# Fourier stage over all 576 tokens at once: no reversed copies through DRAM, one load of each image's rows

## The chip, the cores and the metric

One core of a Trainium2 chip runs the whole program: attention, then a Fourier layer with an MLP, then a gated MLP. The number that counts is the device time of one execution in microseconds (us); three runs of the kernel before took 1231.2, 1236.0 and 1241.24, median 1236.0. Engines are called by the profile's names: PE (TensorE matmul), DVE (VectorE), ACT (ScalarE), POOL (GpSimd) and SP, whose queue issues most DMAs.

## What is computed

The part that the change touches is the mixing at the head of the second layer. `x` is the attention's output, 4 images of 576 tokens by 512 features:

```
X = np.fft.fft(x, axis=1)
X = np.fft.fft(X, axis=2)
u = x + np.real(X).astype(np.float32)
mu, var = mean and variance of u over the features
un = (u - mu) / np.sqrt(var + 1e-06)
x2 = u + np.maximum(un @ w_ch1, 0.0) @ w_ch2
```

The attention before it (4 images, 8 heads, 576 tokens, head size 64, a bias from a small network on the distances) and the gated MLP behind it keep their code.

## The kernel before

**Attention.** `attention_phase` walks 16 head pairs (4 of each image) of 9 units each; a step `d` handles two units. The steps are written as a software pipeline: scores and their maximum at `d`, exponentials one step later, then a split of the probabilities into two fp16 halves (`high` on ACT, `low` on POOL, line 473), a DMA transpose (`turn`, line 485, on SP's queue) three steps later, and the product with v (`back`, line 527) six steps later. In every third step, and in the last three, PE does the transpose instead (`flip`, with a leftover subtraction `flip_low` on DVE). When a pair is done, `store` writes 128 of the 512 features of one image to a DRAM buffer `xd[b]` (lines 572 and 573).

**The Fourier stage's input.** Before the cosine and sine sums over the tokens are taken, token s is added to and subtracted from token 576 - s, so that 289 rows are contracted. [...] Image 2 goes to a tile of its own (`fx`), image 3 reuses image 0's.

**Folds.** `Folds.prep` is the elementwise work of one image, ten steps: sum and difference of the two row sets (lines 781 and 782, POOL and DVE), the same over the features (787), then four groups of 128 columns, each rounded to the matmul's format by ACT (812), with the remainder taken by POOL (813) and DVE (793). `first_folds` starts it while the attention drains, `fft_phase` calls one step of it at a time between matmuls.

**The two contractions.** `stage1` makes one column group of one image with 7 matmuls of 290 columns against the table `tt` (line 887); an image has five groups: `p1` (one column), `pe`, `po`, `me`, `mo`. `second` contracts the features in 12 or 8 matmuls (line 920), `residual` transposes x itself (lines 906 and 908), and two DVE additions write the result into `ut` (lines 924 and 931). `residual` has two PSUM buffers, and each is freed by one of these additions. Both phases stand under `manual_schedule`; the order on each engine is settled when the program is built. Weight blocks of the MLP (`w<-in_w_ch`) are converted in between by `Weights.step`, 8 short DVE instructions for each.

Of the kernel before, what the change touches and what calls it, by code (L numbers as in the profile page):

```python
# [20 lines left out]
DM = 512  # L21
# [32 lines left out]
REV = 14  # L54
# [296 lines left out]
def attention_phase(tc, nc, io, vs, bias, biasl, raw, xd, ident, after, es, right):  # L351
# [4 lines left out]
    vp = right.enter_context(pool(tc, name="vp", bufs=1, side="right"))  # L356
# [69 lines left out]
    def total(u):  # L426
        n, t, h = units[u]
        sc = live.pop(u)
        bv = bias[t // 2][:, t % 2, 2 * pairs[n][1] + h] if t < 4 else biasl[:, pairs[n][1]]
        s = wp.tile([128, S], F32, tag="s", name="s", bufs=SB)  # L430
# [13 lines left out]
        live[u] = s  # L444
# [87 lines left out]
    def finish(u):  # L532
# [3 lines left out]
        if n not in xs:  # L536
            xs[n] = xp.tile([128, 5, 128], F32, tag="x", name="x")
# [26 lines left out]
    def store(u):  # L564
        n, t, h = units[u]
        if t < 4:
            return
# [10 lines left out]
    wp = es.enter_context(pool(tc, name="att", bufs=3))  # L578
    xp = es.enter_context(pool(tc, name="xs", bufs=2))
# [65 lines left out]
def phases(tc, nc, io, vs, low, raw, xd, ident, tables, after, right):  # L645
# [4 lines left out]
    with ExitStack() as es:  # L650
        att = attention_phase(tc, nc, io, vs, bias, biasl, raw, xd, ident, after, es, right)
# [25 lines left out]
LEAD = 2  # L677
F_LOAD = -3
F_WAIT = 2
F_PREP = 1  # L680
F_STEPS = 2
F_MAX = 7
YB = 3
XPLAN = {10: 1, 14: 1, 30: 1, 31: 1, 32: 1}
AFTER = (0,)


def clear(eng, x):

    eng.memset(x[96:128, :, 2], 0.0)  # L690
    eng.memset(x[0:1, 1, 0], 0.0)


def fetch(eng, x, d):


    f = slice(1, DM + 1)
    eng.dma_start(out=x[:, 0, 0:2, f], in_=d[0:256].rearrange("(k p) d -> p k d", p=128))
    yield
    eng.dma_start(out=x[1:128, 1, 0, f], in_=d[577:704])  # L700
    eng.dma_start(out=x[:, 1, 1, f], in_=d[704:832])
    yield
    for y, s in enumerate((256, 832)):
        r = d[s : s + 32].rearrange("(a s) d -> a s d", a=1)
        eng.dma_start(out=x[0:96, y, 2, f], in_=r.to_broadcast([3, 32, DM]))
    eng.dma_start(out=x[96:98, 0, 2, f], in_=d[288:289].to_broadcast([2, DM]))
    yield


def tables(tc, nc, io, es):  # L710

    cp = es.enter_context(pool(tc, name="dft", bufs=1, side="right"))

# [5 lines left out]
    def load():  # L719
        nc.gpsimd.dma_start(out=tt, in_=io["c_t"])  # L720
# [10 lines left out]
class Folds:  # L731
# [5 lines left out]
    SIZE = 2 * 3 * (DM + 2)  # L737
    WORK = 6144

    def __init__(self, tc, nc, xd, xs, work, es):  # L740
        self.tc, self.nc, self.xd, self.es = tc, nc, xd, es
        self.xs = [self.view(x) for x in xs]
        n = 0

        def room(y, f):
            nonlocal n
            n += y * f
            return work[:, n - y * f : n].rearrange("p (y f) -> p y f", y=y)

        self.eo = [room(3, DM) for _ in range(2)]  # L750
        self.pm = room(12, 256).rearrange("p (y z t) f -> p y z t f", y=2, z=2)
# [3 lines left out]
        self.loads = {}  # L755

    def view(self, x):
        return x.rearrange("p (y t f) -> p y t f", y=2, t=3)

    def open(self):  # L760

        p = self.es.enter_context(pool(self.tc, name="ff", bufs=1, side="right"))
        for x in range(2):
            self.hi.append(p.tile([128, 3, DM], F32R, name=f"fhi{x}"))
            self.lo.append(p.tile([128, 2, DM], F32R, name=f"flo{x}"))
        self.xs.append(self.view(p.tile([128, self.SIZE], F32, name="fx2")))

    def load(self, b, eng=None):

        nc, x = self.nc, self.xs[b % 3]  # L770
        if b < 3:
            clear(nc.gpsimd, x)
        if b == B - 1:
            reverse(nc, self.xd, b)
            yield
        yield from fetch(eng or nc.sync, x, self.xd[b])

    def prep(self, b):
        nc, x, f = self.nc, self.xs[b % 3], slice(1, DM + 1)
        eo, pm, hi, lo = self.eo, self.pm, self.hi[b % 2], self.lo[b % 2]  # L780
        nc.gpsimd.tensor_tensor(out=eo[0], in0=x[:, 0, :, f], in1=x[:, 1, :, f], op=ALU.add)
        nc.vector.tensor_tensor(out=eo[1], in0=x[:, 0, :, f], in1=x[:, 1, :, f], op=ALU.subtract)
        yield

        def half(y, z):
            eng = nc.gpsimd if (y, z) == (1, 1) else nc.vector
            eng.tensor_tensor(
                out=pm[:, y, z], in0=eo[y][:, :, 255::-1], in1=eo[y][:, :, 256:512], op=ALU.subtract if z else ALU.add
            )

        def low(g):
            q, r = slice(128 * g, 128 * g + 128), slice(64, 97)
            nc.vector.tensor_tensor(out=hi[r, 2, q], in0=F[r, 2, q], in1=hi[r, 2, q].bitcast(F32), op=ALU.subtract)

        half(1, 0)
        half(1, 1)
        yield
        half(0, 0)
        yield
        half(0, 1)  # L800
        yield
        F = eo[0]
# [3 lines left out]
        for g, (y, z, op, c) in enumerate(((0, 0, ALU.add, 0), (1, 0, ALU.subtract, 128), (0, 1, ALU.subtract, 0), (1, 1, ALU.add, 128))):  # L806
            q = slice(128 * g, 128 * g + 128)
            o = F[:, :, q]
            s = pm[:, y, z]
            nc.vector.tensor_tensor(out=o[:, :, 1:128], in0=s[:, :, up], in1=s[:, :, dn], op=op)  # L810
            nc.vector.tensor_copy(out=o[:, :, 0:1], in_=pm[:, g // 3, z, :, c : c + 1])
            nc.scalar.activation(out=hi[:, :, q], in_=o, func=AF.Copy)
            nc.gpsimd.tensor_tensor(out=lo[:, :, q], in0=o[:, 0:2], in1=hi[:, 0:2, q].bitcast(F32), op=ALU.subtract)
            if g:
                low(g - 1)
            yield
        low(3)
        yield

    def steps(self):  # L820
        for b in range(B):
            for n, _ in enumerate(self.prep(b)):
                self.done = 10 * b + n
# [5 lines left out]


def first_folds(folds):

    def flow():
        yield from folds.load(0)
        for _ in range(F_WAIT):
            yield
        yield from folds.load(1)

    steps = flow()

    def after(n):
        if n == 0:
            folds.open()
        if n >= F_LOAD:
            next(steps, None)
        for _ in range(F_STEPS):
            if n >= F_PREP and folds.done < F_MAX:
                next(folds.flow)
        if n == LAGS[-1] + 1:
            for _ in steps:  # L850
                pass
# [4 lines left out]
def fft_phase(tc, nc, folds, tabs, ut, bank, extra, es):  # L856
# [9 lines left out]
    COS, SIN = (0, 2, 8), (4, 6, 9)  # L866
# [3 lines left out]
    def load(b):  # L870
        for _ in folds.load(b):
            pass

    need(2)
    need(8)
    load(2)
    need(9 + LEAD)

    def stage1(b, nm, col, ncol, t):
# [3 lines left out]
        seq = [(hi[0:98, 2, c], tt[0:98, t[2]])]  # L883
        for k in range(2):
            seq += [(hi[:, k, c], tt[:, t[0] + k]), (hi[:, k, c], tt[:, t[1] + k]), (lo[:, k, c], tt[:, t[0] + k])]
        for n, (st, mv) in enumerate(seq):
            nc.tensor.matmul(out=y[0:ncol, 0:TP], lhsT=st, rhs=mv, start=(n == 0), stop=(n == 6))
# [4 lines left out]
    def first(b, nm):  # L892
        if nm == "p1":
            x = xs[b % 3]
            nc.scalar.activation(out=x[:, :, :, 0:1], in_=x[:, :, :, 256:257], func=AF.Copy)
        need(10 * b + dict(p1=6, pe=6, po=6, me=7, mo=8)[nm])
        stage1(b, nm, *dict(p1=(128, 1, COS), pe=(0, 128, COS), po=(128, 128, SIN), me=(256, 128, COS), mo=(384, 128, SIN))[nm])

    def residual(b, e, y):
        x = xs[b % 3]  # L900
        t = ps_x.tile([128, 2, 512], F32, tag="xs", name="xs")
        for s in range(2):
            col = 257 + e if s else e
            c = slice(col, col + 255, 2)
            for k in range(2):
                nc.tensor.transpose(t[:, s, 128 * k : 128 * k + 128], x[:, y, k, c], ident)
            r = slice(64, 97)
            nc.tensor.transpose(t[:, s, 256:289], x[r, y, 2, c], ident[r, r])
# [20 lines left out]
    def mirror(b, e):  # L929
        o = ut[:, 2 * e : 2 * e + 2, S * b : S * b + S]  # L930
        ends[0] = nc.vector.tensor_tensor(
            out=o[:, :, T2:S], in0=Ds["xr"][:, :, 287:0:-1], in1=Ds["d"][:, ::-1, 287:0:-1], op=ALU.add
# [3 lines left out]

    def step():
        nonlocal count
        count += 1
        next(folds.flow, None)  # L940
# [6 lines left out]
    for b in range(B):  # L947
        for e in range(2):
# [4 lines left out]
            for n, nm in enumerate(group):  # L953
# [12 lines left out]
        if b + 3 < B:  # L966
            load(b + 3)
# [617 lines left out]
def build(tc, io, out):  # L1585
    nc = tc.nc
    with ExitStack() as ctx:
# [9 lines left out]
        xd = [dp.tile([S + S // 2, DM], F32, name=f"xd{b}") for b in range(B)]  # L1597
        n, m = Folds.SIZE, Folds.WORK
# [150 lines left out]
```

## Time and profile before

| | |
|---|---|
| median of 3 runs | 1236.0 us (1231.2 to 1241.24) |
| profiled execution | 1236.24 us, span 1234.4 us |
| bias tables | 0 to about 125 us |
| attention, up to the last scores | about 125 to 423 us |
| drain of the attention and image 0 of the Fourier stage | 423 to 500 us |
| the rest of the Fourier stage | 500 to 568 us |
| MLP | 568 to 1016 us |
| gated MLP | 1016 to 1234 us |
| busy share of the span | PE 87%, DVE 61%, ACT 46%, POOL 35% |

The profile is of one execution, and 1.8 us lie outside its span. Busy shares are averages over stages with different limits: PE is busy for 331 of 336 us in the middle of the MLP, and for 12 of 30 us between 470 and 500. A stage is therefore read from its own stretch.

### The profile page before, as it was taken

Reading aid. Unit: us, or ns where it says so; the run is one execution under the profiler, and the core shown is the slowest. Engines: PE = TensorE matmul, PEld = TensorE weight load, DVE = VectorE, ACT = ScalarE, POOL = GpSimd, SP = SyncE. Lnnn points to the kernel's source line nnn. Section 1 sums busy time; section 2 is a strip of 40 time slices with the busy share of each in tenths; the row PEclk is TensorE's granted clock in tenths of the full one; section 3 lists DMA queues with packets and bytes.
Section 4 is the critical chain, followed back from the end, with each engine's and each line's share of the span. In section 5 each row is a group of like instructions: output and inputs, shape, how many; then the busy total and the mean of one; then the engine's idle time right before and its main releaser. Section 6 shows DMA issues by size and latency. Waiting matters only on the chain.

```text
span 1234.4 us, 25635 instructions
## 1 busy us (share of the span) xinstructions
PE 1069.7 (87%) x10379; PEld 980.0 (79%) x10379; DVE 749.8 (61%) x2099; ACT 565.2 (46%) x1056; POOL 434.8 (35%) x345
## 2 busy tenths in 40 slices
PE   4989898959868625788788999999999999999998
PEld 2778787858857613567787999999999998898997
DVE  5898877748747535867999723423448427534422
ACT  2788888859857501325444312212224324334332
POOL 2667677757756423431555000000005311101010
PEclk7899999989979868778999999999999999999999
DMA  6442198878878762201543000000013200001001
GB/s 146 155 130 87 32 176 173 170 147 166 177 139 171 128 102 82 96 22 52 158 151 119 1 2 1 1 1 1 35 36 127 59 1 1 18 18 43 1 35 43
DMA packets 145642, 98.86 MB, mean 80 GB/s; under 512 B 111476, under 2 KB 125168, under 8 KB 145396
## 3 DMA queue, kind: packets, MB, share of 16 engines
q1 hardware_dynamic: 142656, 89.84, 31.5%
q10 hardware_dynamic: 2724, 5.90, 1.6%
q8 instruction: 81, 1.33, 0.5%
q0 software_dynamic: 144, 1.48, 0.3%
q14 instruction: 37, 0.30, 0.1%
HBM read 60.64 MB, written 11.79 MB: 59 GB/s over the span
## 4 chain that ended last, share of the span: by engine, by line
PE 50%; DVE 20%; DMA 11%; POOL 7%; SPq 4%; ACT 4%; issue 4%; ACTq 0%; POOLq 0%; DVEq 0%
PE h L1297 12%; PE acc L1333 12%; PE psp L1468 5%; DMA pt<-hl 4%; PE pu L1443 4%; PE po L1490 3%; POOL hl L473 3%; PE pv L1391 3%; PE sc L421 3%; DVE wsq L1033 2%; DVE wsq L1038 2%; SPq L485 2%; DVE wsq L1026 2%; PE bps L265 2%; DMA raw<-in_k 2%
## 5 line engine op out<-in xcount | busy, mean ns | idle before, releaser
L1045 POOL TENSOR_TENSOR wl<-wsq,wh 128x512 fp32r<-128x512 f32 x44 | 80.8, 1848 | 342.4 <-DVE w L1219 249.9
L1297 PE MATMUL h<-uh,wl 128*128 128x256 f32 x576 | 164.1, 286 | 11.2 <-POOL wl L1045 11.2
L1333 PE MATMUL acc<-gh,wh 128*128 128x256 f32 x576 | 164.5, 286 | 3.5 <-ACT gh L1301 3.4
L1297 PE MATMUL h<-uh,wh 128*128 128x256 f32 x576 | 163.1, 285 | 4.4 <-ACT uh L1207 3.2
L1333 PE MATMUL acc<-gl,wh 128*128 128x256 f32 x576 | 162.4, 282 | 5.1 <-DVE gl L1302 4.8
L1297 PE MATMUL h<-ul,wh 128*128 128x256 f32 x576 | 163.2, 284 | 0.0
L1333 PE MATMUL acc<-gh,wl 128*128 128x256 f32 x576 | 161.5, 281 | 0.0
L1302 DVE SCALAR_TENSOR_TENSOR gl<-h,gh 128x256 fp32r<-128x256 f32 x144 | 60.4, 421 | 160.4 <-ACT gh L1301 160.2
L527 PE MATMUL po<-vp,pt 128*128 128x65 f16 (+1 forms) x2240 | 96.3, 198 | 63.9 <-DMA pt<-hl 57.4
L1301 ACT ACTIVATE gh<-h 128x256 fp32r<-128x256 f32 x144 | 54.5, 379 | 210.3 <-PE h L1297 210.1
L527 PEld LDWEIGHTS <-pt 128*128 128x128 f16 (+1 forms) x2240 | 82.5, 103 | 79.0 <-DMA pt<-hl 65.3
L1297 PEld LDWEIGHTS h<-uh,wl 128*128 128x128 f32 x576 | 111.3, 193 | 12.7 <-POOL wl L1045 12.6
L473 POOL TENSOR_TENSOR hl<-P,hl 128x1024 f16<-128x1024 f32 x92 | 116.2, 1287 | 8.3 <-issue 5.7
L1297 PEld LDWEIGHTS h<-uh,wh 128*128 128x128 f32 x576 | 111.1, 194 | 5.4 <-ACT uh L1207 3.7
L1333 PEld LDWEIGHTS acc<-gl,wh 128*128 128x128 f32 x576 | 109.8, 191 | 6.8 <-DVE gl L1302 6.5
L1333 PEld LDWEIGHTS acc<-gh,wh 128*128 128x128 f32 x576 | 109.9, 191 | 5.0 <-ACT gh L1301 4.6
L1297 PEld LDWEIGHTS h<-ul,wh 128*128 128x128 f32 x576 | 111.3, 194 | 0.2 <-DVE ul L1208 0.2
L1333 PEld LDWEIGHTS acc<-gh,wl 128*128 128x128 f32 x576 | 109.7, 190 | 0.0
L456 ACT ACTIVATE P<-s,mm 128x576 f32<-128x576 f32 x144 | 103.3, 765 | 8.7 <-DVE mm L449 8.3
L434 DVE CUSTOM_DVE_ANT_0 s<-sc,lowa 128x576 f32<-128x576 f32 x64 | 48.4, 757 | 49.9 <-PE sc L421 48.3
L265 PE MATMUL bps<-g,mask 128*128 128x64 f16 x1152 | 63.6, 199 | 17.3 <-DVE mask L320 11.1
L248 ACT ACTIVATE mask<-pre 128x576 f16<-128x576 f32 x96 | 60.9, 651 | 35.2 <-PE pre L245 34.1
(257 smaller groups left out, 2837.9 us busy)
## 6 DMA issues: line engine op xcount, KB each, us to landing
w<-in_w_ch SPq DMA_DIRECT2D x32, 512.0 KB
vld<-in_v ACTq DMA_DIRECT2D x16, 320.0 KB
raw<-in_v SPq DMA_DIRECT2D x16, 320.0 KB
raw<-in_q SPq DMA_DIRECT2D x16, 288.0 KB
raw<-in_k SPq DMA_DIRECT2D x16, 288.0 KB
xd<-x SPq DMA_DIRECT2D x16, 256.0 KB
w<-in_w_in SPq DMA_DIRECT2D x8, 512.0 KB
out<-o SPq DMA_DIRECT2D x16, 256.0 KB
```

The lines of the kernel that those rows point to most:

```text
L248: nc.scalar.activation(out=m.rearrange("p (x e) -> p x e", x=2), in_=p[:, :, 0:288], func=AF.Sigmoid, scale=1e30)
L265: nc.tensor.matmul(out=full(ps, it // 2)[:, it % 2, :, gi], lhsT=ms[gi][:, 128 * it : 128 * it + 128], rhs=g[:, k], start=(k == 0), stop=( ...
L456: nc.scalar.activation(out=P[:, x], in_=s, func=AF.Exp, bias=mm[:, 1, x : x + 1], scale=1.0)
L473: nc.gpsimd.tensor_tensor(out=hl[:, :, o : o + c], in0=P[:, :, j : j + c], in1=hl[:, :, j : j + c], op=ALU.subtract)
L527: nc.tensor.matmul(out=po[c, t % 4, 0:w], lhsT=pt[:, x, c], rhs=vp[:, j, hh, f : f + w], start=(i == 0), stop=(i == len(seq) - 1),)
L1045: nc.gpsimd.tensor_tensor(out=lo, in0=w[4], in1=hi.bitcast(F32), op=ALU.subtract)
L1297: nc.tensor.matmul(out=h[:, 0:MC], lhsT=st[:, q], rhs=mv[:, k], start=(n == 0), stop=(n == 11))
L1301: nc.scalar.activation(out=gh, in_=h[:, 0:MC], func=AF.Relu)
L1302: nc.vector.scalar_tensor_tensor(out=gl, in0=h[:, 0:MC], scalar=0.0, in1=gh.bitcast(F32), op0=ALU.max, op1=ALU.subtract)
L1333: nc.tensor.matmul(out=acc[d][:, x], lhsT=st[:, q], rhs=mv, start=(i == LAGF and n == 0), stop=(i == len(items) + LAGF - 1 and n == 2),)
L1443: nc.tensor.matmul(out=p[:, 0:CH], lhsT=st[:, q], rhs=mv[:, kk, e], start=(n == 0), stop=(n == 11))
L1468: nc.tensor.matmul(out=p[:, 0:CH], lhsT=st, rhs=mv, start=(n == 0), stop=(n == len(seq) - 1))
```

## The change

`stage1` contracts all 576 tokens in natural order: 4 blocks of 128 rows and one of 64, with 14 matmuls of 290 columns for each column group instead of 7. The fold over tokens, the reversed copies and the loads of reversed rows go. One image is loaded by two DMAs, `[128, 4 x 512]` and `[64, 512]`; image 0 three steps ahead of the attention's end, images 1 and 2 right behind its last step, each into a tile of its own, image 3 three steps later. The last head pair is not stored: its result is written straight into image 3's tile, and only 384 of that image's features are loaded. `prep` has six steps, on DVE and ACT alone. The table has two halves of the old size; the sine half is loaded by a DMA on POOL's queue at the attention's end.

```diff
-REV = 14
...
-def reverse(nc, xd, b):
-    nc.sync.dma_start(
-        out=xd[b][S + 1 : S + S // 2].rearrange("s (z d) -> z s d", z=2),
-        in_=xd[b][S - 1 : S // 2 : -1].rearrange("s (z d) -> z s d", z=2),
-    )
...
-            xs[n] = xp.tile([128, 5, 128], F32, tag="x", name="x")
+            xs[n] = xp.tile([128, 5, 128], F32, tag="x", name="x") if n + 1 < len(pairs) else last
...
-        if t < 4:
+        if t < 4 or n + 1 == len(pairs):
             return
...
-            if u % (9 * NP) == REV and u > REV:
-                reverse(nc, xd, u // (9 * NP) - 1)
...
-F_MAX = 7
-YB = 3
+F_MAX = 9
+YB = 2
...
     def open(self):
         p = self.es.enter_context(pool(self.tc, name="ff", bufs=1, side="right"))
+        self.sin = p.tile([128, 10, TP], F32R, name="sin")
+        self.nc.gpsimd.dma_start(out=self.sin, in_=self.io["c_t"][:, 1])
...
+    def load(self, b):
+        nc, x, d = self.nc, self.xs[b], self.xd[b]
+        n = DM if b + 1 < B else DM - 128
+        f = slice(1, n + 1)
+        nc.sync.dma_start(out=x[:, 0:4, f], in_=d[0:512, 0:n].rearrange("(k p) d -> p k d", p=128))
+        nc.sync.dma_start(out=x[0:64, 4, f], in_=d[512:S, 0:n])
+
+    def prep(self, b):
...
+        for g, op in enumerate((ALU.add, ALU.subtract, ALU.subtract, ALU.add)):
+            z = g // 2
+            s = pm[z]
+            if g % 2 == 0:
+                nc.vector.tensor_tensor(
+                    out=s, in0=x[:, :, 256:0:-1], in1=x[:, :, 257 : DM + 1], op=ALU.subtract if z else ALU.add
+                )
+                yield
...
+            nc.vector.tensor_tensor(out=F[:, :, 1:128], in0=s[:, :, up], in1=s[:, :, dn], op=op)
+            nc.vector.tensor_copy(out=F[:, :, 0:1], in_=s[:, :, c : c + 1])
+            nc.scalar.activation(out=hi[:, :, q], in_=F, func=AF.Copy)
+            nc.vector.tensor_tensor(out=lo[:, :, q], in0=F[:, 0:4], in1=hi[:, 0:4, q].bitcast(F32), op=ALU.subtract)
+            r = slice(0, 64)
+            nc.vector.tensor_tensor(
+                out=hi[64:128, 4, q], in0=F[r, 4], in1=hi[r, 4, q].bitcast(F32), op=ALU.subtract
+            )
             yield
...
     def after(n):
+        if n == F_LOAD:
+            folds.load(0)
         if n == 0:
             folds.open()
+            for b in range(1, B - 1):
+                folds.load(b)
+        if n == 3:
+            folds.load(B - 1)
...
     def stage1(b, nm, col, ncol, t):
...
-        seq = [(hi[0:98, 2, c], tt[0:98, t[2]])]
-        for k in range(2):
-            seq += [(hi[:, k, c], tt[:, t[0] + k]), (hi[:, k, c], tt[:, t[1] + k]), (lo[:, k, c], tt[:, t[0] + k])]
+        seq = []
+        for k in range(4):
+            seq += [(hi[:, k, c], t[:, k]), (hi[:, k, c], t[:, 4 + k]), (lo[:, k, c], t[:, k])]
+        seq += [(hi[:, 4, c], t[:, 8]), (hi[:, 4, c], t[:, 9])]
...
-        if b + 3 < B:
-            load(b + 3)
```

SP's queue at the end of the attention before: `xd_73` to `xd_76` are the DRAM buffers of images 0 to 3, `DMA_TRANSPOSE` is `turn`, `L345` the reversed copy, `L698` to `L706` the loads of image 0.

```order
L485 DMA_TRANSPOSE pt<-hl 128x18x128 x2
L345 DMA xd_75<-xd_75 2x287x256
L485 DMA_TRANSPOSE pt<-hl 128x18x128
L572 DMA xd_76<-x 128x4x128
L573 DMA xd_76<-x 64x128
L698 DMA raw<-xd_73 128x2x512
L700 DMA raw<-xd_73 127x512
L701 DMA raw<-xd_73 128x512
L485 DMA_TRANSPOSE pt<-hl 128x18x128
L705 DMA raw<-xd_73 96x1x512 x2
L706 DMA raw<-xd_73 2x512
```

The same place in the change:

```order
L476 DMA_TRANSPOSE pt<-hl 128x18x128 x3
L563 DMA xd_76<-x 128x4x128
L564 DMA xd_76<-x 64x128
L733 DMA raw<-xd_73 128x4x512
L734 DMA raw<-xd_73 64x512
L476 DMA_TRANSPOSE pt<-hl 128x18x128
L733 DMA lowb<-xd_74 128x4x512
L734 DMA lowb<-xd_74 64x512
L733 DMA lowb<-xd_75 128x4x512
L734 DMA lowb<-xd_75 64x512
```

The reversed copy no longer stands between two transposes, and the last transpose has two loads ahead of it instead of three.

DVE in the change, from image 0's last two column groups to the last result of the attention (`ri`, then `lowb<-po,ri` into image 3's tile) and image 1's first step; `L746` and `L753` to `L758` are the new `prep`:

```order
L753 TENSOR_TENSOR raw<-lowb 128x5x127
L754 COPY raw<-lowb 128x5
L756 TENSOR_TENSOR flo_8300<-raw,fhi_8299 128x4x128
L758 TENSOR_TENSOR fhi_8299<-raw,fhi_8299 64x128
L753 TENSOR_TENSOR lowb<-lowb 128x5x127
L754 COPY lowb<-lowb 128x5
L756 TENSOR_TENSOR flo_8300<-lowb,fhi_8299 128x4x128
L758 TENSOR_TENSOR fhi_8299<-lowb,fhi_8299 64x128
L533 TENSOR_SCALAR ri<-po,vs 128x4
L537 RECIPROCAL ri<-ri 128x4
L541 TENSOR_TENSOR lowb<-po,ri 128x4x64
L746 TENSOR_TENSOR lowb<-lowb 128x1280
```

All of image 0's elementwise work stands ahead of the instruction that frees the attention's last output buffer.

DVE further on, where image 1 and two weight blocks end and the first additions into `ut` (`lowa`) begin:

```order
L975 SCALAR_TENSOR_TENSOR wsq<-w_8791,wsq 128x256 x2
L756 TENSOR_TENSOR flo_8302<-lowb,fhi_8301 128x4x128
L758 TENSOR_TENSOR fhi_8301<-lowb,fhi_8301 64x128
L963 TENSOR_SCALAR wsq<-wsq 128x256 x2
L965 TENSOR_SCALAR wsq<-wsq 128x256 x2
L970 SCALAR_TENSOR_TENSOR wsq<-w_8864,wsq 128x256 x2
L975 SCALAR_TENSOR_TENSOR wsq<-w_8864,wsq 128x256 x2
L859 TENSOR_TENSOR lowa<-xs,d 128x2x289
L866 TENSOR_TENSOR lowa<-xs,d 128x2x287
L746 TENSOR_TENSOR lowb<-lowb 128x1280
```

All of image 1's elementwise work and two weight blocks stand ahead of image 0's first addition, which frees a buffer that PE needs. On PE itself, the groups `p1` and `pe` of image 0 now stand ahead of the attention's last product.

## Rows read from the trace of the kernel before

**Rows 1.** Busy time by stretch: window, length, engines' busy us, PE clock, DMA share, GB/s.

```profile
194.00:229.00 35.00, 30.65 (x422) 28.22 (x421) 26.30 (x88) 28.90 (x42) 26.23 (x21) 0.95 0.89 173
229.00:272.50 43.50, 29.63 (x423) 27.22 (x421) 28.07 (x94) 31.25 (x44) 29.79 (x24) 0.93 0.78 150
306.50:351.00 44.50, 30.30 (x430) 27.63 (x426) 28.48 (x94) 31.23 (x43) 29.79 (x24) 0.93 0.80 148
351.00:385.50 34.50, 30.91 (x415) 28.91 (x416) 23.85 (x79) 26.65 (x37) 22.33 (x17) 0.89 0.86 175
```

**Rows 2.** Timeline of SP's queue: start us, length us; reversed copy, then transpose.

```profile
257.69 0.75 SPq L345 DMA_DIRECT2D xd<-xd  x1
260.37 12.13 SPq L485 DMA_TRANSPOSE pt<-hl  x1
```

**Rows 3.** Timeline of PE; in brackets the idle time before, and what ended it.

```profile
274.64 0.94 PE L527 MATMUL po<-vp,pt 128*128 128x65 f16 x14 [11.05 <-DMA pt<-hl]
...
430.17 0.94 PE L527 MATMUL po<-vp,pt 128*128 128x65 f16 x14 [6.92 <-DMA pt<-hl]
...
461.60 1.30 PE L496 MATMUL turn<-ident,P 128*128 128x128 f32 x5 [13.74 <-DVE pt L510]
```

**Rows 4.** Stretches in which little but one transfer ran, columns as in the first group.

```profile
269.00:272.00 3.00, 0.00 (x0) 0.00 (x0) 0.00 (x0) 0.00 (x0) 0.00 (x0) 0.50 0.14 48
438.00:442.00 4.00, 0.00 (x0) 0.00 (x0) 0.00 (x0) 0.00 (x0) 0.00 (x0) 0.83 0.28 27
```

**Rows 5.** Stretches of the Fourier stage, columns as in the first group.

```profile
500.00:568.00 68.00, 61.13 (x259) 43.74 (x258) 50.83 (x84) 22.88 (x49) 26.79 (x18) 0.83 0.20 61
530.00:551.00 21.00, 18.42 (x66) 12.45 (x67) 17.28 (x27) 5.60 (x12) 9.73 (x7) 0.69 0.10 26
551.00:568.00 17.00, 15.65 (x75) 11.71 (x74) 11.26 (x26) 6.70 (x14) 2.46 (x2) 1.00 0.17 44
```

**Rows 6.** Chain of waits, PE at full clock: start us, length us, what.

```profile
552.40 1.15 PE y L887 x7
553.55 0.23 PE xs L906 x2
...
554.68 1.14 PE y L887 x7
555.82 3.51 PE D L920 x12
...
563.57 1.97 PE D L920 x8
```

**Rows 7.** Timeline of PE within one group of `stage1`.

```profile
552.98 0.43 PE L887 MATMUL y<-tt,fhi 128*128 128x290 f32 x2
553.25 0.30 PE L887 MATMUL y<-tt,flo 128*128 128x290 f32 x1
```

**Rows 8.** Timeline of DVE: single instructions by size.

```profile
465.08 0.29 DVE L510 TENSOR_TENSOR pt<-turn,pt 64x128 f16<-64x128 f32 x1
...
486.11 1.76 DVE L782 TENSOR_TENSOR lowb<-lowb 128x1536 f32<-128x1536 f32 x1 [12.44 <-DMA xd<-x]
...
514.09 0.94 DVE L787 TENSOR_TENSOR lowb<-lowb 128x768 f32<-128x768 f32 x1
515.07 0.56 DVE L810 TENSOR_TENSOR lowb<-lowb 128x381 f32<-128x381 f32 x1
515.54 0.16 DVE L811 COPY lowb<-lowb 128x3 f32<-128x3 f32 x1
...
566.92 0.74 DVE L931 TENSOR_TENSOR lowa<-xs,d 128x574 f32<-128x574 f32 x1
```

**Rows 9.** Groups by line, DVE, 420 to 600 us: count, busy us, mean ns.

```profile
L787 DVE TENSOR_TENSOR lowb<-lowb 128x768 f32<-128x768 f32 x12 | 22.5, 1909 | 0.1
```

**Rows 10.** Timeline of ACT: an instruction of 640 elements.

```profile
437.01 0.70 ACT L497 ACTIVATE pt<-turn 128x640 f16<-128x640 f32 x1 [0.32 <-PE turn L496]
```

**Rows 11.** DMA issues: the table's load, KB, us from issue to landing.

```profile
tt<-in_c_t POOLq DMA_DIRECT2D x1, 1450.0 KB, 8.0
```

More of the change, by code (lines that the diff above doesn't have):

```diff
@@ L340, in bias_phase, with attention_phase @@
             evict(blk - 1)
-def reverse(nc, xd, b):
-    nc.sync.dma_start(
-        out=xd[b][S + 1 : S + S // 2].rearrange("s (z d) -> z s d", z=2),
-        in_=xd[b][S - 1 : S // 2 : -1].rearrange("s (z d) -> z s d", z=2),
-    )
-def attention_phase(tc, nc, io, vs, bias, biasl, raw, xd, ident, after, es, right):
-    vp = right.enter_context(pool(tc, name="vp", bufs=1, side="right"))
+def attention_phase(tc, nc, io, vs, bias, biasl, raw, xd, ident, last, after, es, right):
+    vp = es.enter_context(pool(tc, name="vp", bufs=1))
     e1 = right.enter_context(ExitStack())
@@ L639, in attention_phase, with phases @@
                 store(u)
-            if u % (9 * NP) == REV and u > REV:
-                reverse(nc, xd, u // (9 * NP) - 1)
+        if d == nd:
+            e1.close()
         after(d - nd)
-def phases(tc, nc, io, vs, low, raw, xd, ident, tables, after, right):
+def phases(tc, nc, io, vs, low, raw, xd, ident, tables, last, after, right):
     n = 2 * H * S
@@ L650, in phases @@
     with ExitStack() as es:
-        att = attention_phase(tc, nc, io, vs, bias, biasl, raw, xd, ident, after, es, right)
+        att = attention_phase(tc, nc, io, vs, bias, biasl, raw, xd, ident, last, after, es, right)
         ready = False
@@ L719, in load @@
     def load():
-        nc.gpsimd.dma_start(out=tt, in_=io["c_t"])
+        nc.gpsimd.dma_start(out=tt, in_=io["c_t"][:, 0])
         yield
@@ L731, with __init__ @@
 class Folds:
[L737 to L751, printed above, removed]
+    SIZE = 5 * (DM + 1)
+    STEPS = 6
+    def __init__(self, tc, nc, io, xd, xs, work, temps, es):
+        self.tc, self.nc, self.io, self.xd, self.es = tc, nc, io, xd, es
+        self.xs = [x.rearrange("p (t f) -> p t f", t=5) for x in xs]
+        self.pm = [w.rearrange("p (t f) -> p t f", t=5) for w in work]
+        self.temps = [t.rearrange("p (t f) -> p t f", t=5) for t in temps]
         self.hi, self.lo = [], []
@@ L754, in __init__, with last @@
         self.flow = self.steps()
-        self.loads = {}
-    def view(self, x):
-        return x.rearrange("p (y t f) -> p y t f", y=2, t=3)
+    def last(self):
+        return self.xs[B - 1][:, :, DM - 127 : DM + 1]
     def open(self):
         p = self.es.enter_context(pool(self.tc, name="ff", bufs=1, side="right"))
+        self.sin = p.tile([128, 10, TP], F32R, name="sin")
+        self.nc.gpsimd.dma_start(out=self.sin, in_=self.io["c_t"][:, 1])
         for x in range(2):
-            self.hi.append(p.tile([128, 3, DM], F32R, name=f"fhi{x}"))
-            self.lo.append(p.tile([128, 2, DM], F32R, name=f"flo{x}"))
-        self.xs.append(self.view(p.tile([128, self.SIZE], F32, name="fx2")))
@@ L768, in load @@
[L768 to L774, printed above, removed]
-            yield
[L776 to L802, printed above, removed]
-        up, dn = slice(1, 128), slice(255, 128, -1)
[L806 to L818, printed above, removed]
@@ L822, in steps @@
             for n, _ in enumerate(self.prep(b)):
-                self.done = 10 * b + n
+                self.done = self.STEPS * b + n
                 yield
@@ L828, in need, with ahead @@
             next(self.flow)
+    def ahead(self, n):
+        if self.done < n:
+            next(self.flow, None)
 def first_folds(folds):
[L833 to L839, printed above, removed]
     def after(n):
+        if n == F_LOAD:
+            folds.load(0)
         if n == 0:
             folds.open()
-        if n >= F_LOAD:
-            next(steps, None)
+            for b in range(1, B - 1):
+                folds.load(b)
+        if n == 3:
+            folds.load(B - 1)
         for _ in range(F_STEPS):
[L847 to L851, printed above, removed]
+            if n >= F_PREP:
+                folds.ahead(F_MAX)
     return after
@@ L865, in fft_phase @@
     xs, need = folds.xs, folds.need
-    COS, SIN = (0, 2, 8), (4, 6, 9)
+    COS, SIN = tt, folds.sin
     ys, Ds = {}, {}
     ends = [None, None]
[L870 to L877, printed above, removed]
+    need(folds.STEPS - 1)
     def stage1(b, nm, col, ncol, t):
@@ L904, in residual @@
             c = slice(col, col + 255, 2)
[L905 to L908, printed above, removed]
+            for n, (k, r) in enumerate(((2, 128), (3, 128), (4, 64)) if y else ((0, 128), (1, 128), (2, 33))):
+                nc.tensor.transpose(t[:, s, 128 * n : 128 * n + r], x[0:r, k, c], ident[0:r, 0:r])
         Ds["xr" if y else "xf"] = t
@@ L931, in mirror @@
         ends[0] = nc.vector.tensor_tensor(
-            out=o[:, :, T2:S], in0=Ds["xr"][:, :, 287:0:-1], in1=Ds["d"][:, ::-1, 287:0:-1], op=ALU.add
+            out=o[:, :, T2:S], in0=Ds["xr"][:, :, 33:320], in1=Ds["d"][:, ::-1, 287:0:-1], op=ALU.add
         )
     count = 0
+    limit = 2 * folds.STEPS - 1
     def step():
@@ L939, in step @@
         count += 1
-        next(folds.flow, None)
+        folds.ahead(limit)
         for _ in range(XPLAN.get(count, 0)):
@@ L961, in fft_phase @@
                     step()
+            if e == 0:
+                limit += folds.STEPS
             if not group:
@@ L1596, in build @@
         dp = ctx.enter_context(tc.tile_pool(name="dram", bufs=1, space=bass.MemoryType.DRAM))
-        xd = [dp.tile([S + S // 2, DM], F32, name=f"xd{b}") for b in range(B)]
-        n, m = Folds.SIZE, Folds.WORK
-        folds = Folds(tc, nc, xd, [raw[:, 0:n], more[:, m : m + n]], more, right)
+        xd = [dp.tile([S, DM], F32, name=f"xd{b}") for b in range(B)]
+        n, o = Folds.SIZE, 3 * Folds.SIZE
+        folds = Folds(
+            tc, nc, io, xd,
+            [raw[:, 0:n]] + [more[:, n * b : n * b + n] for b in range(B - 1)],
+            [more[:, o : o + 1280], more[:, o + 1280 : o + 2560]],
+            [raw[:, n : n + 640], more[:, o + 2560 : o + 3200]],
+            right,
+        )
         with ExitStack() as e1:
             e1.enter_context(tc.manual_schedule())
-            phases(tc, nc, io, vs, (low, more), raw, xd, tabs[2], load, first_folds(folds), right)
+            phases(tc, nc, io, vs, (low, more), raw, xd, tabs[2], load, folds.last(), first_folds(folds), right)
         tail(tc, nc, io, folds, tabs, low, right, out, ctx)
```

56 lines of the change are left out of this document (23 added, 33 removed).

## The prediction

> **What bounds the kernel now.** I began with the busy time by stretch, to see which stages can move. The change leaves the bias tables, the MLP and the gated MLP as they are, so I read only the attention's stretches and the Fourier stage, then SP's queue and PE's idle times where two equal stretches differ, and last the single instructions that the new code is made of.
>
> In the attention, stretches of two head pairs take 35.0 and 34.5 us where no reversed copy falls into them, and 43.5 and 44.5 where one does [rows 1]. The engines' busy times hardly differ, so the surplus is waiting. SP's queue shows where: the transpose issued behind the reversed copy takes 12.13 us [rows 2], and PE stands still for 11.05 us until its output lands [rows 3]. Meanwhile the DMA engines move 48 GB/s at a busy share of 0.14 [rows 4], against 175 at 0.86 in an undisturbed stretch [rows 1]: the copy runs on a few engines, and the transpose waits for them. The load of 127 reversed rows does the same behind the attention's end: 27 GB/s, PE idle throughout [rows 4].
>
> Between 423 and 500 us PE does little: 6.92 us of waiting for a transpose behind the third reversed copy, and 13.74 us for DVE, which sits in image 0's first fold until the last rows land [rows 3]. From 500 on PE is busy for 61.1 of 68 us, at a mean clock of 0.83 [rows 5]. So three things bound this part: slow transfers, then waits, then PE at a clock that the waits keep low.
>
> **The reversed copies.** Without them I take 43.5 - 35.0 and 44.5 - 34.5 off, **18.5 us** for those of images 0 and 1. The bounds are 0, if other transfers fill the gap, and twice PE's wait, 22; I take the difference of whole stretches, since it contains everything that followed. The third copy's 6.92 us lie in the drain and are counted there. The last score work ended at 430.17 - 6.92 = 423.2, and now ends at 404.7.
>
> **The drain.** Image 0's two loads are 1.18 MB; at 175 GB/s [rows 1] they take 6.7 us, and they are issued about 5 us before 404.7, so they land near 407. The 64-row load is the unknown: at the 27 GB/s of the 127-row load [rows 4] its 128 KB would take 4.9 us by itself and the landing would be near 412. I take 407, since the slow load has a row count that nothing even divides. The Trainium skill, "DMA: Bandwidth & Descriptors" (Why a DMA increments its semaphore by 16 and not by 1), says that a copy is spread over the largest number of engines up to 16 that divides the outer dimension; it gives all 16 to 64 rows, one to 127 and two to the reversed copy. By it the landing is 407, by the bound 412.
>
> DVE then carries a serial chain. Prices come from a line through 381, 768 and 1536 elements [rows 8]: 0.81 us for 635, 0.69 for 512, 1.49 for 1280. One column group costs 0.81 + 0.16 (copy) + 0.70 (ACT rounds, DVE waits [rows 10]) + 0.69 + 0.29 = 2.65, with two handovers about 2.75; an image costs 2 x 1.49 + 4 x 2.75 = **14.0 us**, of which DVE is busy for 10.8. DVE ends the attention's older work near 410, then image 0's 14.0, the remainders of four flips between them (4 x 0.98 = 3.9) and the division of one result (0.8): 428.7. Only then does PE get its last output buffer.
>
> PE next does that product, `po`, a residual, `me`, the first 12 matmuls of `second`, `mo`, and the second residual, at the low clock at first, and reaches the third residual near 445. That needs image 0's first addition, which stands on DVE behind image 1 (14.0), the last divisions (1.6) and two weight blocks of 8 short instructions (5): 428.7 + 20.6 = **449**. So there is a new wait of some 4 us on PE, and it is in the sum.
>
> **PE from there.** Seven matmuls take 1.15 us [rows 6], one more takes (553.25 - 552.98) / 2 = 0.135 [rows 7], so a group of 14 takes 1.15 + 7 x 0.135 = 2.09. An image: 5 x 2.09 + 3.51 + 1.97 + 4 residuals of 1.13 = 20.5 us, where it was 15.8; the doubling costs 4 x 4.7 = **19 us**. Of 82.0 us, 16.2 are done by 449 (three groups, 9.95 for the first half of image 0), and 65.8 remain.
>
> The stretch 500 to 568 us says how far from dense PE works here. At these prices it held 15 groups, 7 parts of `second`, 13 residuals and a small sum, 51 us of work in 68: a factor of 1.33. Where no fold ran, 551 to 568 us, it was 15.65 busy of 17 at clock 1.00 [rows 5], 1.09. The waits of the worse part came from rows that landed late and from DVE instructions beside POOL's: the 768-element instruction took 1.91 us on average instead of 0.94 [rows 8, 9]. Both are gone: 5.9 MB from 400 on, at 175 GB/s, are in by about 435, each image ahead of its fold, and POOL keeps only weight remainders. DVE's load of 10.8 + 1.5 x 2 for an image fits beside 20.5 on PE. I take **1.12**, nearer to the clean part, since some waits for ACT's rounding will stay. 449 + 65.8 x 1.12 = 522.7, and 2.1 for the last additions gives 524.8. Before, the last one ended at 567.7 [rows 8].
>
> **Sum.** 1236.24 - (567.7 - 524.8) = **1193 us** for a profiled execution of 1236.24 us, which is within 0.3 of the median of the three runs. What follows the stage is taken unchanged: its weight blocks are as many and stand in the same places.
>
> Ends of my own case: factor 1.09, image 0's first addition 4 us earlier and 2 us more in the attention give 1185; factor 1.33 gives 1207; both errors on DVE's chain add 5. So 1180 to 1210.
>
> **Rivals.**
>
> *The attention does not get faster* (12%). DMA is busy for 0.86 to 0.89 of an undisturbed stretch [rows 1], so it may be bound there anyway. Against it: the surplus is a time of low DMA activity. It gives 1193 + 18.5 = 1212.
>
> *The sine table comes late* (7%). `po` of image 0 needs it near 429, and POOL issues it near 405, while DVE works without a pause. The one such load took 8.0 us [rows 11], so it has 16 us to spare. If it landed only 8.0 us after DVE's chain, at 436.7, PE would lose about 6 us, most of the wait counted above with it: 1199. The Trainium skill, "SBUF — State Buffer" (SBUF: two separate sides), names the mechanism: descriptors of DMAs issued from GpSimd are written over a port that VectorE can lock. No run here shows it, and the chance stays small.
>
> *PE stays at half clock, and the kernel is slower* (6%). The doubled contraction pays only if PE runs it at 2.4 GHz. From 530 to 551 us, with a fold on DVE in each half image, the granted clock averaged 0.69 [rows 5]. If every half image of the new stage held a wait for DVE's in-order chain (DVE waits for ACT, ACT for PE's groups, PE for DVE's addition), PE could remain at 1.2 GHz: 65.8 x 2 = 131.6, the stage would end at 449 + 131.6 + 2.1 = 582.7, and the time would be **1251**. It decides against the change where the factor passes (565.6 - 449) / 65.8 = 1.77. For it: that clock, and three engines that now hand one group to each other. Against it: the longest stretch of dense work between two waits grows by a third, and DVE needs 14 of 20 us.
>
> **Numbers.** Forecast 75%, rivals 12, 7 and 6%. The time of the likeliest is 1193; 1176 to 1216 takes in the first two rivals and the bounds. About 1%, 12 us, is what a measurement of this kernel tells from no change: faster is below 1224, slower above 1248. The forecast and the first two rivals lie below, except where the first meets the factor 1.33 (2%, within 1%). Half clock gives 5% slower and 1% in between. Faster 0.92, same 0.03, slower 0.05.
>
> **What would show it.** Right: stretches of two pairs of 34 to 35 us throughout; no transpose on SP's queue above 6 us; the last scores near 405; the first addition into `ut` near 449 and the last near 525; groups of 14 matmuls at 2.1 us; a clock above 0.9 from 455 on; POOL without folds. Wrong: a wait of PE for the sine table; PE waiting for DVE's additions in every half image; a mean clock below 0.8 in the stage; a gap between the last addition and the MLP's first matmul that differs from before by more than 3 us.

## The result, and the profile after

The changed kernel takes **1188.0 us** (median of 4 runs, 1184.9 to 1189.4), the kernel before 1236.4 in the same comparison: a ratio of **0.961**, interval 0.956 to 0.965. Ten runs of the changed kernel, six of them on another chip, have a median of 1186.9. The profiled execution took 1184.93 us with a span of 1183.1. The forecast was 1193, so the size is right to 5 us. But one price in its working, 19 us for the doubled contraction, is one that this stage doesn't pay, as the experiments show.

First the attention. Busy time by stretch of two head pairs, columns as in [rows 1]:

```profile
225.57:260.00 34.43, 28.10 (x369) 25.85 (x368) 22.74 (x78) 27.07 (x38) 24.96 (x20) 0.90 0.87 177
260.00:295.00 35.00, 31.30 (x434) 29.37 (x431) 26.72 (x89) 30.19 (x42) 26.79 (x21) 0.95 0.86 172
295.00:330.10 35.10, 32.51 (x465) 29.91 (x464) 28.72 (x95) 30.54 (x44) 27.13 (x21) 1.00 0.90 170
330.10:364.30 34.20, 29.01 (x418) 26.57 (x417) 25.84 (x85) 28.58 (x40) 25.88 (x21) 1.00 0.87 177
```

All four are as short as the undisturbed ones of before. The DMA share is 0.86 or more in each, where it was 0.78 and 0.80 in the two stretches with a copy. SP's queue, columns as in [rows 2]:

```profile
251.81 8.14 SPq L476 DMA_TRANSPOSE pt<-hl  x2
...
262.90 3.83 SPq L476 DMA_TRANSPOSE pt<-hl  x1
```

Two transposes take 8.14 us together where one behind a copy took 12.13 [rows 2]. PE's sum of waits for their output, 125 to 400 us (total us, times, longest):

```profile
PE po L518 <- DMA pt<-hl: 24.8, 21, 3.5
```

Before, from 125 to 425 us, it was 40.5 us in 17 times, the longest 11.5. From the loads of q at 228.88 and 385.53 us to those at 225.57 and 364.29, the stretch with both copies fell by 156.65 - 138.72 = 17.9 us. Another 3.3 us (228.88 - 225.57) lie ahead of the first copy, where the change does nothing: two executions differ by that much.

Then the drain and the Fourier stage, columns as in [rows 5]:

```profile
400.00:445.00 45.00, 28.91 (x315) 24.82 (x313) 38.51 (x91) 14.50 (x24) 2.30 (x3) 0.81 0.61 178
...
445.00:516.20 71.20, 70.53 (x387) 55.34 (x386) 39.15 (x71) 23.61 (x47) 3.82 (x3) 1.00 0.08 23
```

PE is busy for 70.53 of 71.2 us, at the full clock throughout; the rows of before say 61.1 of 68 at 0.83. The waits that are left stand ahead of 445. PE's timeline, idle time and releaser in brackets:

```profile
412.36 1.30 PE L487 MATMUL turn<-ident,P 128*128 128x128 f32 x5 [4.74 <-DVE pt L501]
...
426.03 1.55 PE L518 MATMUL po<-vp,pt 128*64 128x65 f16 x28 [2.26 <-DVE lowb L541]
...
429.43 0.85 PE L823 MATMUL y<-sin,fhi 128*128 128x290 f32 x2 [1.84 <-ACT y L826]
...
437.82 0.85 PE L823 MATMUL y<-tt,fhi 128*128 128x290 f32 x2 [3.69 <-ACT y L826]
```

The last two weren't foreseen: neither of the two PSUM buffers for `y` is free, because ACT has not yet evicted an older one. ACT's own timeline says why:

```profile
436.73 0.74 ACT L755 ACTIVATE fhi<-raw 128x640 fp32r<-128x640 f32 x1 [2.92 <-DVE raw L754]
437.37 0.40 ACT L826 ACTIVATE y<-y 128x290 f32<-128x290 f32 x1
```

In ACT's program order the eviction stands behind a rounding of image 1, and that waits 2.92 us for DVE's fold. DVE's timeline gives the first addition into `ut` and the end of the stage (before, 498.88 and [rows 8]):

```profile
446.51 0.76 DVE L859 TENSOR_TENSOR lowa<-xs,d 128x578 f32<-128x578 f32 x1 [1.63 <-ACT d L857]
...
515.45 0.74 DVE L866 TENSOR_TENSOR lowa<-xs,d 128x574 f32<-128x574 f32 x1
```

The last addition ends at 516.2, before at 567.7: 51.5 us, all of the difference of the two profiled executions (51.3). What follows is unchanged: 666.9 us to the end of the span, before 666.7.

A dense PE looks like the bound of the stage. The chain of waits (start us, length us, what), over one image, shows something else:

```profile
468.76 0.77 DVE lowa L859
...
469.58 1.41 PE xs L843 x6
470.98 1.94 PE y L823 x14
472.93 1.97 PE D L855 x8
474.92 0.67 ACT d L857
475.60 0.76 DVE lowa L859
476.37 0.73 DVE raw L753
...
477.21 0.75 ACT fhi L755
477.98 0.69 DVE flo L756
...
486.61 0.82 DVE lowb L753
...
487.54 0.75 ACT fhi L755
488.32 0.69 DVE flo L756
489.02 0.28 DVE fhi L758
489.34 0.77 DVE lowa L859
```

From one addition to the same addition an image later, 468.76 to 489.34, the chain runs through PE for 5.3 us only. The other 15 are DVE's additions, sums and four column groups, in its program order, with ACT's rounding inside each group. Busy time over that image, columns as in [rows 1]:

```profile
468.76:489.34 20.58, 20.42 (x115) 16.11 (x116) 13.26 (x23) 6.50 (x13) 0.00 (x0) 1.00 0.00 1
```

This loop is 20.6 us long, and PE has 20.4 us of work in it. Two loops of equal length run side by side.

### The profile page after: what moved, and what is told of

Same layout as the page of the kernel before. It is cut to its first block, busy times and chain, and to the rows that moved or that the text cites. A ratio compares the mean times of both kernels' runs of the same rounds, so it can differ in the third digit from the quotient of the medians.

```text
span 1183.1 us, 25832 instructions
## 1 busy us (share of the span) xinstructions
PE 1078.8 (91%) x10519; PEld 990.8 (84%) x10519; DVE 737.4 (62%) x2107; ACT 568.1 (48%) x1056; POOL 394.5 (33%) x316
## 4 chain that ended last, share of the span: by engine, by line
PE 52%; DVE 23%; DMA 9%; POOL 6%; ACT 5%; issue 3%; SPq 2%; ACTq 0%; POOLq 0%; DVEq 0%
PE h L1234 13%; PE acc L1270 12%; PE psp L1405 5%; DMA pt<-hl 4%; PE pu L1380 4%; PE po L1427 4%; POOL hl L464 3%; PE pv L1328 3%; DVE wsq L970 2%; DVE wsq L975 2%; DVE wsq L963 2%; PE sc L412 2%; DMA raw<-in_k 2%; PE y L823 2%; DVE bt L308 2%
## 5 line engine op out<-in xcount | busy, mean ns | idle before, releaser
L518 PE MATMUL po<-vp,pt 128*128 128x65 f16 (+1 forms) x2240 | 95.5, 198 | 30.8 <-DMA pt<-hl 24.8
L425 DVE CUSTOM_DVE_ANT_0 s<-sc,lowb 128x576 f32<-128x576 f32 x80 | 60.6, 757 | 28.4 <-PE sc L412 24.8
L264 PE MATMUL bps<-g,mask 128*128 128x64 f16 x1152 | 61.3, 195 | 17.5 <-DVE mask L319 11.5
```

What stands on the lines that cost most here:

```text
L264: nc.tensor.matmul(out=full(ps, it // 2)[:, it % 2, :, gi], lhsT=ms[gi][:, 128 * it : 128 * it + 128], rhs=g[:, k], start=(k == 0), stop=( ...
L425: nc.vector.tensor_tensor_reduce(out=s.rearrange("p (x e) -> p x e", x=2), in0=sc[:, :, 0:288], in1=bv.rearrange("p (x e) -> p x e", x=2), ...
L518: nc.tensor.matmul(out=po[c, t % 4, 0:w], lhsT=pt[:, x, c], rhs=vp[:, j, hh, f : f + w], start=(i == 0), stop=(i == len(seq) - 1),)
```

## Experiments

Each kernel was timed beside the kernel before on the same chip. Ratios are to the kernel before; the changed kernel's were 0.9606 and, repeated on the chip of the last four runs, 0.9608.

A yardstick for them: the attention's length differs by some 9 us between profiled executions of the changed kernel and its variants, so the Fourier stage is also measured within a profile, from the last load of q to the start of the last addition into `ut`. That takes 151.2 and 151.4 us in two profiles of the changed kernel and 181.4 in the kernel before.

### The reversed copies alone

`reverse` copies 287 rows of an image, 289 to 575, in reverse order to the end of the image's DRAM buffer, as two halves of 256 columns; the copies of images 0 to 2 are issued 14 units into the next image. The kernel before without these three (its folds then read rows in natural order):

```diff
-            if u % (9 * NP) == REV and u > REV:
-                reverse(nc, xd, u // (9 * NP) - 1)
```

> The kernel before without the reversed copies of images 0 to 2 (left out: the folds of these three images then read rows in natural order in their place, by loads of the same shapes; the copy of image 3 stays). Theory, a transpose queued behind a copy on two DMA engines: the two stretches of 43.5 and 44.5 us shrink to 35, and the 6.92 us behind the third copy go, so 1236 - 18.5 - 7 = 1211 us (1208 to 1219, since what the third copy cost may come back in the drain). Rival, the attention is bound by DMA bytes or by an engine anyway: 1233 to 1237.

Measured 1207.2 us (1204.6 to 1210.4) beside 1238.0: 0.977, interval 0.972 to 0.982. The 30.8 us are somewhat more than the most that the theory allowed (28), and the rival falls. And the other way round, the same lines and `reverse` put into the changed kernel:

> The changed kernel with the reversed copies of images 0 to 2 put back in the attention, at the places where the kernel before has them; nothing reads what they write. Theory: two stretches of two pairs become some 9 us longer each, and the third copy costs up to 7 us, so 1188 + 18.5 = 1206.5 without and 1213.5 with the third. Rival, the gain of the change is all in the Fourier stage and the attention is bound otherwise: 1187 to 1191.

Measured 1217.3 us (1210.1 to 1222.9), 0.985 (0.979 to 0.991): 29 to 32 us more than without. In its SP queue and on PE the old picture is back:

```profile
261.80 0.73 SPq L345 DMA_DIRECT2D xd<-xd  x1
264.53 11.76 SPq L485 DMA_TRANSPOSE pt<-hl  x1
...
278.44 0.94 PE L527 MATMUL po<-vp,pt 128*128 128x65 f16 x14 [10.49 <-DMA pt<-hl]
```

Copies and Fourier stage add up: about 30 us for the first, some 19 to 21 for the second, in either order.

The profiles say what each copy costs. The stretch from the load of q at 228.88 (before) to that at 385.53, which holds the first two copies, is 17.0 us shorter without them, and 21.0 longer in the changed kernel with them. The transpose behind the third copy ends 42.6 us after the last load of q, and 31.0 in the changed kernel (385.53 and 364.29):

```profile
413.73 14.35 SPq L485 DMA_TRANSPOSE pt<-hl  x1
...
385.63 9.66 SPq L476 DMA_TRANSPOSE pt<-hl  x3
```

Of these 11.6 us not all reach the stage's end: by the yardstick the third copy costs 7.6 us in the kernel before (181.4 against 173.8) and 10.1 in the changed one (161.2 against 151.2).

The Fourier stage's own gain lies in the drain. From the last load of q to the first addition the kernel before without these copies takes 108.7 us and the changed kernel 82.2; from there to the start of the last addition they take 65.1 and 68.9. In that drain of the kernel before DVE waits 14.38 and 18.68 us for rows to land, as in [rows 8]; in the changed kernel it has no such wait. No run changes the loads alone, so this part of the cause is read from profiles and not tested.

### The copy's bytes or its engines

```diff
-    nc.sync.dma_start(
-        out=xd[b][S + 1 : S + S // 2].rearrange("s (z d) -> z s d", z=2),
-        in_=xd[b][S - 1 : S // 2 : -1].rearrange("s (z d) -> z s d", z=2),
-    )
+    d = xd[b]
+    for n, m in ((0, 272), (272, 15)):
+        nc.sync.dma_start(out=d[S + 1 + n : S + 1 + n + m], in_=d[S // 2 + 1 + n : S // 2 + 1 + n + m])
```

The edit stands in `reverse`, so it changes the copy of image 3 too; the rows keep their order.

> The kernel before with each copy of 287 rows made as 272 rows plus 15, rows in forward order (the values are then wrong in order, the bytes are the same), so that the outer dimension is one that 16 divides. Theory, the small number of engines is what costs, not the bytes: nearly all of the gain of leaving the copies out, 1211 to 1220 us, and no transpose above 6 us. Rival, the 0.57 MB read and written by each copy cost the time wherever they run: 1230 to 1237.

Measured 1205.7, 1208.7 and 1211.0 us, and 1224.1 in a fourth run, which was the profiled one; the ratio is 0.978 (0.972 to 0.984, the first three), as without the copies. SP's queue behind the first copy:

```profile
256.10 1.22 SPq L347 DMA_DIRECT2D xd<-xd  x2
258.27 3.17 SPq L484 DMA_TRANSPOSE pt<-hl  x1
```

The transpose takes 3.17 us behind the same 0.57 MB. So the bytes cost nothing that these runs can tell; the layout of the copy cost about 30 us. The edit changes three things at once, the outer dimension, the order of the rows and the length of one run (512 features for 256), and no run separates them. The load of 127 rows reads forward and is slow too [rows 4], which speaks for the outer dimension. No view counts engines; an estimate from the busy share of 0.14 in [rows 4] is 0.14 x 16 = 2.2 for the copy. This agrees with the rule of the Trainium skill, "DMA: Bandwidth & Descriptors" (Why a DMA increments its semaphore by 16 and not by 1), that a DMA runs on the largest number of engines up to 16 that divides its outer dimension.

### The doubled contraction

```diff
-        for k in range(4):
+        for k in range(0, 4, 2):
             seq += [(hi[:, k, c], t[:, k]), (hi[:, k, c], t[:, 4 + k]), (lo[:, k, c], t[:, k])]
-        seq += [(hi[:, 4, c], t[:, 8]), (hi[:, 4, c], t[:, 9])]
+        seq += [(hi[:, 4, c], t[:, 8])]
```

> The changed kernel with 7 of each group's 14 matmuls (left out: half of the contraction over tokens; everything else is done). Theory, the stage is bound by PE from the first addition on and the doubling costs its full length: 20 groups x 7 x 0.135 = 19 us less, 1169 us. Rival, DVE's folds and sums of an image (14 of 20.5 us) come close to binding and take part of it back: 1174 to 1180. Second rival, the shorter groups leave PE at half clock in places: 1180 or more.

Measured 1185.5 us (1184.8 to 1185.8), 0.959 (0.954 to 0.964). **The theory fell**: half of the groups' matmuls are gone, and the time stays within 2.5 us; the yardstick is 151.5, as with all of them. The time lies where the second rival put it. One image, from addition to addition, columns as above:

```profile
472.40:493.53 21.13, 17.51 (x79) 12.48 (x79) 13.25 (x22) 6.49 (x13) 0.00 (x0) 0.92 0.00 0
```

and PE's timeline at its start:

```profile
473.21 1.43 PE L843 MATMUL xs<-ident,lowb 128*128 128x128 f32 x6 [3.54 <-DVE lowa L859]
```

The period is no shorter, 21.1 us. PE now waits for DVE's addition, and the granted clock is 0.92 in this image, which takes more back. Only the end of the stage, where no folds are left, gets shorter: from image 2's first addition (at 489.34 in the changed kernel, here at 493.53) to the end of the last it takes 23.9 us instead of 26.9, and the two images before it lose about as much (45.4 us for 42.8). Two causes were open: DVE's loop, or the clock. The next kernel has the same matmuls and smaller folds, of three token tiles in five:

```diff
-                    out=s, in0=x[:, :, 256:0:-1], in1=x[:, :, 257 : DM + 1], ...
+                    out=s[:, 0:5:2], in0=x[:, 0:5:2, 256:0:-1], in1=x[:, 0:5:2, 257 : DM + 1], ...
...
```

> Half of the contraction as in the run with 7 matmuls in a group, and the folds made for three of the five token tiles only (left out: the folds of the other two, which nothing then reads). Theory, the run with 7 matmuls gained nothing since a loop through DVE's in-order queue (additions, sums, two column groups per half image, ACT's rounding in between) is as long as PE's 20.5 us an image: with some 4 us less of it per image the time falls to 1165 to 1178. Rival, PE at half clock is what holds that kernel: no change, 1183 to 1188.

Measured 1171.8 us (1164.3 to 1175.9), 0.946 (0.942 to 0.950): 14 us less, from shorter instructions of DVE and ACT alone. One image takes 16.25 us:

```profile
462.91:479.16 16.25, 15.78 (x80) 11.79 (x79) 10.06 (x23) 5.64 (x13) 0.00 (x0) 1.00 0.00 0
```

The clock is back at 1.00, although PE's work is the same: the loop came first, and the clock followed it. How the loss divides between the two isn't measured. Nor is all of the gain in the loop: by the yardstick it is 14.8 us (136.7 for 151.5), of which 6.8 come ahead of the first addition, in the drain, and 7.9 behind it. Smaller folds with all 14 matmuls were not run. And the changed kernel with more on DVE:

```diff
-            if g % 2 == 0:
+            for _ in range((2 if b > 1 else 1) if g % 2 == 0 else 0):
                 nc.vector.tensor_tensor(
                     out=s, in0=x[:, :, 256:0:-1], in1=x[:, :, 257 : DM + 1], ...
                 )
+            if g % 2 == 0:
                 yield
```

> The changed kernel with DVE's instruction of 1280 elements done twice, for images 2 and 3 only: 2 x 2 x 1.48 = 5.9 us more on DVE while PE runs the stage. Theory of the loop: DVE has no slack there, and the time grows by 4 to 6 us, 1192 to 1194. Theory of the prediction, DVE's 14 us fit beside 20.5 us of PE with room to spare: 1187 to 1189.

Measured 1191.8 us (1191.3 to 1193.3), 0.964 (0.961 to 0.967): some 4 us more by the ratios, though the intervals overlap. The yardstick is clearer, 156.6, which is 5.3 us more for 5.9 added. In its profile the period is

```profile
471.57:495.29 23.72, 22.01 (x114) 16.93 (x114) 16.24 (x24) 6.49 (x13) 0.00 (x0) 0.93 0.00 1
```

3.1 us longer for 2.96 us added. DVE is busy for 13 of 20.6 us in the changed kernel and has no slack, since its idle time is spent waiting for others within the same loop.

### POOL beside the folds

```diff
-            nc.vector.tensor_tensor(out=lo[:, :, q], in0=F[:, 0:4], ...
+            nc.gpsimd.tensor_tensor(out=lo[:, :, q], in0=F[:, 0:4], ...
```

> The changed kernel with the remainder of four token tiles (the 128x512 subtraction) on POOL, where the kernel before has its remainders. Theory, work on POOL beside DVE's folds is what made the stage of the kernel before loose: DVE's instructions that overlap it grow (1.91 us for 0.94 before), and the stage loses up to 5 us, 1190 to 1195. Rival, the contention was small or lay elsewhere: DVE's chain gets shorter by 4 x 0.69 an image and PE stays the bound, 1184 to 1189.

Measured 1186.3 us (1182.4 to 1191.6), 0.960 (0.956 to 0.963), yardstick 151.3: no difference, so the theory's 1190 to 1195 missed and the rival's range holds. The growth itself is there. Groups by line, DVE, 400 to 520 us (count, busy us, mean ns):

```profile
L753 DVE TENSOR_TENSOR lowb<-lowb 128x635 f32<-128x635 f32 x8 | 11.5, 1434 | 0.1
...
L753 DVE TENSOR_TENSOR raw<-lowb 128x635 f32<-128x635 f32 x8 | 6.6, 820 | 0.5
```

Every second column group overlaps POOL's remainder, and its first instruction takes 1.43 us on average instead of 0.82. Over one image:

```profile
470.07:490.75 20.68, 20.44 (x115) 16.12 (x115) 12.56 (x19) 6.49 (x13) 5.14 (x5) 1.00 0.00 1
```

DVE was spared four remainders of 0.69 us, 2.8 in all, and is busy for only 0.7 us less than in the changed kernel (12.56 for 13.26): its other instructions grew by about 2. What was left gained nothing, as PE has 20.4 us of work in the image.

### A version that beats both

```diff
-F_MAX = 9
+F_MAX = 5
```

> The changed kernel with F_MAX 5 for 9: image 1's folds no longer stand among the drain's work but one by one behind the groups of image 0. Theory, PE's waits of 1.84 and 3.69 us for the evictions of y come from ACT, where they stand behind roundings of image 1 that wait for DVE: both go, and the stage begins up to 5 us earlier, 1183 to 1186. Rival, image 1's folds then come late, and PE waits for them at image 1's first group: 1187 to 1193.

Measured **1180.4 us** (1174.8 to 1186.1), 0.9545 (0.952 to 0.958). PE's waits for `y` are gone from its profile, and the yardstick is 145.7, against 151.2 and 151.4. The gain is in the drain: the first addition starts 74.1 us after the last load of q, in the changed kernel 82.2. Three more tries were run beside a repeat of the changed kernel:

> The changed kernel again, unaltered, as the base for the three runs on the same chip: 1185 to 1190 us.

Measured 1185.1 us (1182.4 to 1192.9).

> F_MAX 5 as before, and the folds of image 0 spread over more iterations of the drain (F_PREP 0, F_STEPS 1 for 1 and 2), so that the remainders of the last transposed tiles do not stand behind four column groups. Theory, PE's waits of 4.7 and 2.3 us for DVE in the drain go, and the first addition comes earlier: 2 to 6 us below F_MAX 5 alone, 1175 to 1180. Rival, image 0's folds end as much later as the tiles come earlier, and the time is that of F_MAX 5 alone: 1180 to 1183.

> F_MAX 5 and the remainder of four token tiles on POOL. Theory of the loop: with F_MAX 5 DVE sets the first images' period (22.2 us from addition to addition, against 20.6), so 0.69 us less per group on DVE brings it back to PE's 20.5: 2 to 4 us below F_MAX 5 alone, 1176 to 1179. Rival, DVE's instructions grow beside POOL (0.82 to 1.43 us in the run with POOL's remainders) and give it back: 1180 to 1184.

> All three edits together: F_MAX 5, F_PREP 0, F_STEPS 1, remainders on POOL. If both theories hold, 1171 to 1178; if only one does, 1176 to 1180; if neither, 1180 to 1184.

Measured 1180.0, 1181.7 and 1180.7 us (ratios 0.954, 0.956, 0.955). None adds anything to F_MAX 5 that is clear of noise, though all stay below the repeat; the yardsticks are 144.0, 145.0 and 147.5. The theories that foresaw more missed; the first of the three times lies on the border between theory and rival. An image takes 22.0 us from addition to addition in the first, 22.0 in the second and 22.2 in the third, as with F_MAX 5 alone:

```profile
467.82:490.01 22.19, 21.37 (x112) 16.48 (x113) 13.26 (x23) 6.49 (x13) 0.00 (x0) 0.92 0.00 1
```

That is longer than either loop of the changed kernel. PE waits 1.3 to 2.6 us for DVE's addition at its start, and the granted clock is 0.92 in all four. Time won in the drain is in part spent there.

## Why the prediction was right, and where it was wrong

- **Copies, -18.5 us for two**: 17.9. The mechanism, a copy whose layout holds up the transpose behind it, is shown by three runs; that few engines are the reason is an estimate from busy shares. The third copy was somewhat under-priced: 6.9 us of it were counted in the drain, and the profiles give 7.6 to 10.1.
- **The last scores** ended at 400.2, not 404.7, and most of the difference is the 3.3 us ahead of the first copy, which are luck. Counted from the last scores, the first addition came after 46.3 us, later than the 44.3 of the forecast.
- **Drain**: DVE began image 0 at 406.9 (predicted 410) and finished it, with the division, at 426.0 (428.7). A column group took 2.7 us (2.75), the sum 1.49. DVE didn't wait for the rows, as taken.
- **The new wait of 4 us for image 0's first addition**: not there. The addition came at 446.5 (449) and waited for PE's product. The waits stood 7 to 16 us ahead of the place foreseen (445), on ACT's order, 1.84 and 3.69 us, and F_MAX 5 took them away. The sum was about right, the place and the cause were wrong: luck.
- **PE's prices** from 445 on: groups of 14 at 1.94 to 2.10 us (2.09), 3.51 and 1.97 for `second`, 1.12 to 1.18 for residuals (1.13). All within 0.15 us.
- **The factor of 1.12**: this is the term that was mis-sized. 67.6 us passed from the first addition to the last but 2.1, against 65.8 of work: 1.03, 6 us of the 8 that the forecast was too high. And the step behind it failed: "DVE's load of 10.8 + 1.5 x 2 for an image fits beside 20.5 on PE" compared busy times, where the loop through DVE, ACT and PE counts. That loop is 20.6 us; that PE needs 20.5 is a coincidence of sizes. Nor did contention with POOL show as the cause of the looseness before: brought back in part (the remainders, not the sums of whole row sets), it cost nothing. By rows of before, additions an image apart stand at 519.20 and 542.10, 22.9 us against 15.8 of PE's work; in that image DVE waits 4.66 us for rows:

```profile
528.20 1.76 DVE L782 TENSOR_TENSOR lowb<-raw 128x1536 f32<-128x1536 f32 x1 [4.66 <-DMA raw<-xd]
```

So late rows, as the prediction said, and DVE's loop may both have bound it there; no run tests that in the kernel before.

- **"The doubling costs 19 us"**: here it costs 2.5 or less, since the loop is as long without it. Only with smaller folds as well does the stretch from the first addition to the last get shorter, 60.6 us for 68.9. In the 19 us every matmul that PE is spared was counted as time won.
- **Rivals.** An attention that stays as it is: refuted by both directions of the copies. The sine table: issued at 407.2 and landed 11.3 us later, 11 us ahead of `po`, which waited for ACT instead. Half clock: 1.00 from 445 on, as forecast; the runs with waits in the loop show where it would have come from (0.81 and 0.92 in two images with 7 matmuls).
- **What follows the stage**: unchanged, as taken.

## What to carry to other kernels

Price a stage in which engines hand one item around as the longer of two lengths: the densest engine's work, and the loop from one hand-over to the same one an item later, through every in-order queue on the way. That is a lower end: where the two miss each other by a little, as with F_MAX 5, waits and the clock add to it. Busy shares show neither slack nor bound there: DVE at 64% had none, and PE at 99% could lose a third of its matmuls for nothing. Where a transfer delays others on its queue, try the same bytes in another layout before removing them, as with the 272 rows here; that alone was worth most of what the rewrite gained in the attention.

## What was not expected of the hardware

A copy of 0.57 MB within DRAM cost nothing visible beside attention work at a DMA share of 0.89 to 0.90, laid out as 272 + 15 rows, and 8 to 11 us each as two halves. DVE's 635-element instruction took 0.82 us alone and 1.43 on average in the column groups that overlap POOL's subtraction.
